# A long-convolution and linear-attention kernel: two blocks of high rows summed by accumulating transfers, numerators scaled straight from PSUM, one-bank spectra tiles, new order lists

## The chip, the cores and the metric

One core of a Trainium2 chip runs the whole kernel. The metric is device time of one execution in microseconds (us). A core has five engines with queues of their own: TensorE (PE, matrix products into PSUM), VectorE (DVE), ScalarE (ACT), GpSimd (POOL) and SyncE (SP, which only issues transfers). Each works through its queue in order and waits on semaphores for the others. SBUF is the working memory with 128 partitions; PSUM holds TensorE's results in banks of 512 fp32 columns.

## The reference

Two independent halves, written side by side into one output of 2048 x 896.

```python
def _A_ref(x, wqkv, w_phi, wo):            # x: 1 x 2048 x 448, 16 heads of 28
    q, k, v = ...                          # x @ wqkv, split into heads
    pq, pk = q @ w_phi, k @ w_phi          # by head
    phi_q = concat(softmax(pq), softmax(-pq))
    phi_k = concat(softmax(pk), softmax(-pk))
    kv, z = einsum("bhsf,bhsd->bhfd", phi_k, v), phi_k.sum over s
    num = phi_q @ kv
    den = phi_q . z + 1e-6
    return (num / den, heads joined) @ wo

def _B_ref(u, A_re, A_im, B_re, B_im, C_re, C_im, log_dt, Dskip):   # u: 1 x 2048 x 448, 256 states
    dt = exp(log_dt); logdA = dt * (A_re + 1j * A_im); dB = dt * (B_re + 1j * B_im)
    P = exp(logdA[:, :, None] * l)         # l = 0 .. 2047, rounded to bfloat16
    K = einsum("dn,dnl,dn->dl", C, P, dB).real
    y = irfft(rfft(pad(u)) * rfft(pad(K)))[:2048]
    return y + u * Dskip
```

## The kernel before

**Convolution kernel K.** The 448 channels go in eight chunks of 56 channels (k = 0..7). A power P at position l is a product of a low and a high factor. For the low rows (W, 50 of them) a chunk's angles are multiplied on TensorE, ScalarE takes Exp of the damping (`dampings`) and Sin of the angle (`rotations`) from PSUM, and VectorE multiplies them (`damp`). The high rows (U, 32 of them, real and imaginary part each) are made on VectorE in `hi_tables` from H (four rows) by complex products with stored powers PW: rows 8 to 11 by PW[256], rows 4 to 7 and 12 to 15 by PW[128], then rows 16 to 23, 24 to 27 and 28 to 31 by PW[512] = (cosine part, sine part). A product with PW[512] is three VectorE instructions: one that multiplies each source row by both parts into a scratch tile t2 (its width is four times the rows' number times 112 columns), a subtraction and an addition. `build_k` multiplies U and W on TensorE in two halves of 112 small matmuls each, and a copy brings each half to SBUF (Ts). `table(k)` is damp and build of chunk k. U, W and E have two buffers, taken in turn by k.

**Spectra.** `scatter_k` moves finished rows of K by many small transfers into Kt; `kernel_spectrum` multiplies them by DFT tables on TensorE (units ks0, ks1, ks2 for three groups of channels: chunks 0 to 3, 4 to 5, 6 to 7). `signal_spectrum` does the same for u in two halves of the sequence: each of 16 steps fills a two-bank PSUM tile "arg" with two results of 448 columns, one copy of 896 columns brings both to SBUF, and transfers write them to DRAM. For the second half of u, one sum of mirrored rows is made by an accumulating transfer on GpSimd's queue (`accum_op`).

**Convolution.** `conv_group` multiplies the spectra of a group on VectorE, `inverse` transforms back on TensorE, copies bring the result to SBUF, and SP writes it out.

**Attention.** `key_pair` and `key_end` make the sums over keys. `query(sc, ...)` handles 512 queries: Exp of the projections, denominators (SC holds their scaled reciprocals, by head), then for each of four blocks of 128 (units q0.0 to q3.3) the numerators in PSUM, their product with SC into `on`, a transpose that adds the two halves, the output projection, and a store. In blocks sc 0 and 1 the product with SC reads PSUM on VectorE. In blocks 2 and 3 (`late`) ScalarE first copies the numerators to SBUF as bfloat16, and VectorE multiplies there by a bfloat16 SC.

**Order.** Every piece of work is a unit with a number in order of the program text and a planner's price for each engine that can do it. The order of all units, with the engine of each, stands in a list written out by hand (`ORDER`: "48A" is unit 48 on ScalarE), and the PSUM tag of each PSUM tile in `PLACES` (a: "arg", two banks; k: "kb"; m: "mm", one bank; two buffers each). The prices are used by nothing at run time. Many copies may run on ScalarE or VectorE; the list says which.

The lines that profile rows name: 347 is VectorE's products and sums (`tt`), 360 ScalarE's activations, 364 its copies (`acopy`), 370 copies on either engine, 380 matmuls, 395 transfers, 709 the negation in `damp`, 842 and 845 reciprocals.

Of the kernel before, what the change touches and what calls it, by code (L numbers as in the profile page):

```python
# [23 lines left out]
N_EARLY = 2  # L24
# [18 lines left out]
HI = ([32 * a for a in range(16)] + [512 + 64 * a for a in range(8)] + [1024 + 128 * a for a in range(8)])  # L43
# [21 lines left out]
def _dft_tables():  # L65
# [27 lines left out]
    for hh in range(4):  # L93
# [3 lines left out]
ORDER = ("0A 48A 3S 1S 2S 4S 8G 23G 13S 25P 46P 36P 30P 32P 47P 44P 29P 17G 193G 27P 49V 50V 53V 51V 192S 19G 52V 54P 55V "  # L97
         "56P 58P 59V 43P 60P 57A 67A 65V 61V 64A 63A 62A 26P 66A 31P 82P 40P 28P 80P 68V 83V 6S 72A 71A 81V 173P 174V "
         "167P 151P 168V 152V 157P 158V 169P 185S 14S 170V 5S 153P 154V 194V 20G 155P 41P 42P 45P 7S 9S 156V 34P 35P 171P "
         "15S 86P 195V 73V 75A 74A 172A 69A 87A 196P 76V 33P 84P 85A 78A 21S 88P 197P 91P 93V 97P 90V 198A 89V 92V 113V "  # L100
         "98V 202P 203P 123P 94P 121P 12S 199S 201G 200G 111A 110A 22G 208P 209P 11S 112V 99V 124A 204A 77A 96V 122V 95V "
         "117V 101V 100V 210A 119P 220P 120A 205S 206G 207G 125P 39P 126A 115A 214P 159P 163P 165P 166A 161P 164A 160A "
         "162A 116V 215P 221P 118A 103V 147P 415P 148V 211S 212S 213S 222A 216A 135P 145P 435P 146A 102V 79V 438A 418A "
         "417A 437A 136V 105V 440P 232P 443A 104V 70V 233P 143P 144V 18S 10S 16S 129P 420P 421P 127P 130V 106V 442A 451P "
         "141P 107V 128V 191G 224G 223S 225S 422A 234A 424A 423A 142V 260P 179P 425P 181P 137P 180V 182V 114A 441P 175P "
         "426V 138V 109V 108V 236G 218S 283G 436P 282A 444A 133P 268A 266A 176A 439A 416P 275A 277A 278A 419A 279A 272A "
         "149P 273A 271A 134V 284V 427P 131P 431P 150V 428V 432V 139P 132V 140V 445P 286V 446V 447P 219G 183G 190G 184G "
         "217G 430P 434P 429P 433P 285V 452V 456P 287V 448V 289V 288V 290V 261A 263A 281A 280A 264A 262A 267A 274A 276A "
         "226P 227P 455P 269A 265A 270A 459V 228A 238P 239P 460P 244P 450P 458A 457A 462A 463A 461P 449P 465P 246A 248A "
         "464A 454P 254A 257A 258A 247A 231G 230S 229S 240A 291V 292V 293V 294V 466V 364G 188G 235S 186S 259A 256A 467P "  # L110
         "453P 480P 296V 295V 300P 468V 297V 483A 253A 482A 356V 299V 298V 475P 478A 309A 477A 301A 249A 471P 472V 485P "
         "363S 339S 237S 469P 340V 486V 342V 487P 470P 488V 341V 252A 304A 251A 312A 302A 474P 245A 306A 476P 365V 255A "
         "479A 343V 481P 484A 315A 303A 250A 307A 310A 627P 491P 473P 358V 345V 344V 492V 311A 630A 313A 314A 308A 621P "
         "177P 626P 623A 305A 624A 629A 628A 178A 489P 346V 493P 316P 321A 337A 241G 324A 642P 490P 242G 366G 622P 645A "
         "326A 320A 329A 325A 322A 333A 317A 318A 243S 189G 357V 338A 319A 336A 328A 327A 330A 373P 374P 334A 335A 331A "
         "332A 631P 347V 323A 625V 349V 348V 375A 359P 350V 632V 377G 352V 351V 551V 553A 360A 361P 367P 368P 369A 353V "
         "511P 529A 533A 530A 514A 362A 513A 526A 525A 633P 552V 516A 522A 515A 532A 385P 521A 528A 523A 386P 354V 355V "
         "535V 512A 518A 517A 524A 531A 527A 519A 520A 554P 634V 371G 537V 536V 538V 372S 378S 534S 376S 387A 540V 539V "
         "541V 555V 556P 557A 646P 379P 380P 649A 648A 542V 543V 544V 545V 495P 501A 370S 505A 510A 641P 635P 494P 637P "
         "636P 643A 504A 644A 507A 509A 496A 381V 651P 546V 547V 638V 558P 653P 548V 652V 550V 549V 654V 598V 503A 560A "  # L120
         "569A 508A 640P 657P 639P 498A 506A 570A 497A 667P 563A 670A 597S 383S 658V 600V 599V 655P 647P 564A 562A 650A "
         "499A 502A 565A 662P 389G 390S 388S 614V 571A 500A 559A 568A 665A 573A 661P 659P 681P 656P 666P 572A 664A 663A "
         "683A 561A 687P 660P 567A 566A 574P 669A 668A 684A 671P 596A 588A 576A 578A 601V 616V 603V 615V 602V 690V 604V "
         "672V 586A 677P 673P 605V 674V 607V 606V 617P 678V 619P 581A 594A 595A 575A 583A 589A 608V 584A 593A 580A 577A "
         "579A 585A 582A 618V 686P 609V 620A 591A 587A 590A 592A 682P 688A 685A 397P 398P 384G 382G 610V 763V 391P 392P "
         "399A 819P 689A 393A 675P 676P 691P 723P 679P 611V 764V 831A 612V 613V 824A 830A 692V 827A 821A 832A 834A 829A "
         "693P 765V 766P 825A 680P 747V 748V 749V 694V 750V 752V 751V 767V 753V 746S 768P 823A 820A 754V 769V 816S 790G "
         "775G 828A 826A 833A 822A 756V 755V 395S 778S 396S 402G 738A 732A 724A 697P 730A 731A 739A 744A 891P 403P 404P "
         "696P 698V 700P 882P 791S 745A 740A 695P 699P 734A 742A 757V 726A 737A 759V 758V 704V 760V 705V 761V 762V 727A "
         "725A 741A 729A 728A 743A 736A 733A 735A 702V 409P 410P 885P 893A 892A 883A 774G 400G 394G 859V 860V 861V 886A "  # L130
         "887A 884A 888P 889A 890A 703V 706V 862V 701V 405A 941P 894P 935P 858S 813S 401S 781S 411A 943A 942A 900P 901P "
         "938P 932P 908P 909P 936A 937A 939A 793G 940A 934A 933A 864V 863V 865V 895V 896V 897V 898V 899V 902V 903P 916P "
         "904A 917P 910V 911P 912A 707P 715A 712A 713A 722A 809S 788S 716A 717A 817G 721A 944P 38P 866V 407G 772S 811S "
         "918V 905P 924P 925P 406G 408G 789G 800G 777G 1282S 802G 945V 946V 947V 770G 714A 926V 906A 709A 786S 795S 187S "
         "776S 818S 808S 710A 720A 718A 719A 711A 708A 919P 1171P 913P 1165P 948V 867V 949V 950P 951P 914A 875V 920A 1172A "
         "1173A 1167A 1166A 907S 810S 927P 958P 959P 921P 922A 928A 952V 835P 804S 960V 876V 37P 961P 801S 836A 1219P 953P "
         "839A 954A 929P 974P 414S 787S 915S 798S 796G 806G 815G 807G 975P 844A 930A 814G 783S 782S 955P 855A 877V 785S "
         "773G 797G 779G 780S 812S 803S 771G 805G 799G 878P 868V 837A 845A 853A 843A 842A 840A 850A 962V 848A 784S 841A "
         "838A 857A 849A 852A 846A 851A 854A 869V 847A 856A 880P 976V 966P 967P 871V 870V 1038V 923S 879A 956A 872V 874V "
         "873V 968V 982P 1168P 1162P 1093P 881A 1039V 1022V 1040V 1220A 991A 1170A 1169A 1221A 1216P 1225P 1164A 1023V "  # L140
         "1024V 1222P 1163A 1107A 1218A 987A 1174P 1175V 1217A 994A 1041P 1104A 1108A 1096A 1098A 1101A 1099A 1025V 1176V "
         "1283S 957S 1021S 1270S 931S 1276S 794S 986A 792S 1227A 1223A 1105A 995A 993A 992A 1226A 1095A 989A 997A 1102A "
         "996A 988A 1043P 1027V 1156V 1026V 1042V 1028V 1177V 1029V 1031V 1271S 413S 1030V 1103A 1277S 1272P 963P 1044A "
         "1100A 1178V 1288S 1032V 964V 1033V 1224A 1034V 1106A 983A 985A 990A 984A 1278P 1279V 1273A 1189P 1190P 977P "
         "1274P 1280P 1094A 1132G 412G 1097A 998P 1035V 1179V 978A 1191A 1281A 1086S 1081S 1054G 1068G 1062G 1053S 1058S "
         "965S 1087S 1036V 1037V 1275V 1133V 1059G 1294S 1017A 1295S 1052S 1289S 1056G 1051G 1091G 1084S 1071G 1300S 1079S "
         "1092S 1228P 1229V 1018A 1016A 1007A 1001A 969P 1003A 999A 1284P 1285A 1135V 1134V 970V 971P 1180P 1004A 1002A "
         "972A 1015A 1011A 1072G 1075G 1065G 1286P 1161S 1067S 1000A 1014A 1008A 1230V 1061G 1049G 1082G 1066G 973S 1306S "
         "1077S 1301S 1136V 979P 1192V 1137V 1138V 1287V 1055G 1046G 1073G 1080G 1139V 1149V 1290P 24P 1181P 1012A 980A "
         "1291A 1010A 1231V 1019A 1006A 1009A 1005A 1020A 1013A 1193P 1296P 1297A 1182A 1292P 1207P 1298P 1151A 1208P "  # L150
# [144 lines left out]
def kernel(  # L295
# [104 lines left out]
    oEND = oF + 61672  # L400
    oT2 = oEND + 4096
    DSK = sb("DSK", [128, D_MODEL], BF16, oDSK)
    PID = sb("PID", [128, 8, 128], BF16, oPID)
    H = sb("H", [128, 4, 2, NCOL], BF16, oH)
    AT = sb("AT", [128, 2, NCOL], BF16, oAT)
    TH = sb("TH", [128, 2, NCOL], BF16, oTH)
# [729 lines left out]
```

## Time and profile before

| | us |
|---|---|
| median of 3 runs | 296.07 (295.61 to 296.17) |
| the profiled execution, its own time | 295.46 |
| its span, first to last instruction | 293.7 |
| VectorE idle before its first instruction | 4.66 |
| VectorE's last convolution step ends | 283.9 |
| TensorE's last matmul ends, about | 290 |

The profile's mean of an instruction is its length from start to end; neighbours on one engine overlap, so a queue's progress is read from start to start. The parts in busy time are those of the engines' compute; waiting and issuing do not count. TensorE ran at a mean granted clock of 0.986. The transfer engines are 10% to 50% busy for most of the span and fuller in the first 25 us and after 200 us:

```profile
PEclk9899999999999999999999999999999989999999
DMA  6985602364003210100432223547886747695033
```

Each digit is one fortieth of the span, in tenths: the clock granted to TensorE, and the mean busy share of 16 transfer engines.

### The profile page before, as it was taken

What the parts mean: (1) busy time and instruction counts of PE and PEld (TensorE: products, weight loads), DVE (VectorE), ACT (ScalarE), POOL (GpSimd) and SP (SyncE); (2) the same over time, 40 slices, a digit from 0 to 9 for tenths busy, and PEclk for the clock granted to TensorE, in tenths of its full rate; (3) what the DMA queues carried; (4) which work ended last, traced back from release to release, by engine and by line L of the source; (5) the groups of instructions that cost most, each with busy time, mean ns of one, the idle gap of its engine ahead of it and who ended that gap; (6) DMA issues with size and microseconds to landing.
All of it is one profiled execution on the core that took longest, in us unless ns stands there. A gap on an engine that the chain in (4) does not pass through costs nothing.

```text
span 293.7 us, 10074 instructions
## 1 busy us (share of the span) xinstructions
PE 252.4 (86%) x4280; PEld 203.5 (69%) x4280; DVE 275.4 (94%) x334; ACT 249.6 (85%) x535; POOL 70.6 (24%) x119
## 2 busy tenths in 40 slices
PE   7688979987988888899789898968678899989994
PEld 2445666775777757868457676957577789879984
DVE  2799999999999999999999999999999999999980
ACT  3999999999999999999999999999999467533421
POOL 4013003412010200000737300089400099000000
PEclk9899999999999999999999999999999989999999
DMA  6985602364003210100432223547886747695033
GB/s 185 283 251 143 192 11 57 101 198 58 7 13 88 58 40 0 33 7 4 83 80 49 41 53 96 123 91 198 296 241 204 253 102 192 171 303 195 2 127 125
DMA packets 40727, 34.91 MB, mean 119 GB/s; under 512 B 22314, under 2 KB 37921, under 8 KB 40555
## 3 DMA queue, kind: packets, MB, share of 16 engines
q1 hardware_dynamic: 35641, 30.37, 35.8%
q0 software_dynamic: 4160, 3.89, 6.8%
q8 instruction: 33, 0.54, 0.7%
q10 hardware_dynamic: 882, 0.02, 0.2%
q14 instruction: 11, 0.09, 0.1%
HBM read 24.02 MB, written 7.34 MB: 107 GB/s over the span
## 4 chain that ended last, share of the span: by engine, by line
ACT 36%; DVE 36%; PE 13%; issue 6%; DMA 5%; SPq 3%; ACTq 0%; DVEq 0%
DVE sbuf L347 30%; ACT sbuf L360 28%; ACT sbuf L370 5%; PE mm L380 5%; PE kb L380 4%; PE arg L380 4%; DMA sbuf<-in_A_wqkv_dram 3%; DVE sbuf L370 3%; SPq L395 3%; ACT L360 2%; DMA sbuf<-sbuf 2%; DVE sbuf L351 1%; DVE sbuf L842 1%; ACT sbuf L709 1%; DVE sbuf L845 0%
## 5 line engine op out<-in xcount | busy, mean ns | idle before, releaser
L380 PEld LDWEIGHTS <-sbuf 128*32 128x32 bf16 (+4 forms) x4056 | 190.7, 119 | 78.5 <-issue 38.4
L347 DVE TENSOR_TENSOR sbuf<-sbuf 128x896 bf16<-128x896 bf16 (+9 forms) x213 | 221.1, 1079 | 2.3 <-ACT sbuf L364 0.7
L380 PE MATMUL mm<-sbuf 128*32 128x50 bf16 (+11 forms) x1901 | 110.4, 261 | 18.1 <-ACT sbuf L360 6.0
L360 ACT ACTIVATE sbuf<-arg 128x224 bf16<-128x224 f32 (+5 forms) x302 | 121.2, 664 | 0.3 <-PE arg L380 0.2
L380 PE MATMUL kb<-sbuf 128*32 128x50 bf16 (+9 forms) x1457 | 81.7, 247 | 7.5 <-issue 2.6
L380 PE MATMUL arg<-sbuf 128*128 128x112 bf16 (+4 forms) x698 | 69.4, 249 | 7.9 <-ACT sbuf L360 4.7
L395 POOL DMA_DIRECT2D sbuf<-sbuf x77 | 46.5, 633 | 103.8 <-issue 38.1
L370 ACT CAST sbuf<-mm 128x448 bf16<-128x448 f32 (+4 forms) x53 | 33.9, 671 | 11.1 <-PE mm L380 7.0
L370 ACT CAST sbuf<-kb 128x448 bf16<-128x448 f32 (+3 forms) x46 | 27.9, 645 | 15.7 <-PE kb L380 14.8
L395 POOL DMA_DIRECT2D SUd<-sbuf x23 | 16.7, 726 | 72.7 <-ACT sbuf L370 69.8
L360 ACT ACTIVATE sbuf<-mm 112x512 bf16<-112x512 f32 x46 | 28.1, 711 | 0.1
L370 ACT CAST sbuf<-arg 128x896 bf16<-128x896 f32 (+2 forms) x27 | 19.4, 747 | 6.4 <-PE arg L380 4.4
L360 ACT ACT_TABLE_LOAD x14 | 18.0, 1283 | 1.4 <-PEq L1120 1.2
L360 ACT ACTIVATE sbuf<-sbuf 128x896 f32<-128x896 f32 (+3 forms) x13 | 12.6, 1013 | 1.9 <-DMA sbuf<-in_B_log_dt_dram 1.9
L347 DVE TENSOR_TENSOR sbuf<-arg,sbuf 128x896 bf16<-128x896 f32 (+1 forms) x10 | 9.7, 988 | 0.1
L364 ACT CAST sbuf<-arg 128x896 bf16<-128x896 f32 x8 | 8.3, 1052 | 1.0 <-PE arg L380 0.9
L347 DVE TENSOR_TENSOR sbuf<-mm,sbuf 128x896 bf16<-128x896 bf16 (+1 forms) x15 | 8.8, 593 | 0.1
L796 PEld LDWEIGHTS <-sbuf 112*128 112x128 bf16 x128 | 7.4, 97 | 2.1 <-issue 1.7
L796 PE MATMUL mm<-sbuf 112*128 112x112 bf16 x112 | 7.8, 212 | 1.1 <-ACT sbuf L370 0.6
L364 ACT CAST sbuf<-sbuf 128x1792 bf16<-128x1792 f32 (+1 forms) x5 | 7.2, 1430 | 0.0
L360 ACT ACTIVATE sbuf<-kb 112x512 bf16<-112x512 f32 x12 | 7.0, 667 | 0.0
L370 DVE CAST sbuf<-arg 128x224 bf16<-128x224 f32 (+1 forms) x4 | 2.2, 560 | 4.8 <-ACT sbuf L370 4.8
(39 smaller groups left out, 82.2 us busy)
## 6 DMA issues: line engine op xcount, KB each, us to landing
sbuf<-const SPq DMA_DIRECT2D x36, 224.0 KB
sbuf<-const SPq DMA_DIRECT2D x6, 512.0 KB
sbuf<-in_B_u_dram SPq DMA_DIRECT2D x6, 448.0 KB
sbuf<-in_A_x_dram SPq DMA_DIRECT2D x4, 448.0 KB
out_dram<-sbuf SPq DMA_DIRECT2D x16, 112.0 KB
sbuf<-SUd SPq DMA_DIRECT2D x1, 1792.0 KB
sbuf<-SUd SPq DMA_DIRECT2D x2, 896.0 KB
out_dram<-sbuf SPq DMA_DIRECT2D x8, 224.0 KB
```

The lines of the kernel that those rows point to most:

```text
L347: lambda: nc.vector.tensor_tensor(out=at(out_), in0=at(a), in1=at(b), op=op), [whose(a), whose(b)], [out_])
L351: lambda: nc.vector.scalar_tensor_tensor(out=at(out_), in0=at(a), scalar=sc, in1=at(b), op0=op0, op1=op1),
L360: lambda: nc.scalar.activation(at(out_), at(a), func, scale=scale, bias=bias),
L364: plan.add({"ACT": 0.09 + count(out_) * 0.833e-3}, lambda: nc.scalar.copy(at(out_), at(a)), [whose(a)], [out_])
L370: lambda e: (nc.scalar.copy if e == "ACT" else nc.vector.tensor_copy)(at(out_), at(a)), [whose(a)], [out_])
L380: nc.tensor.matmul(out_, lhsT=lhsT, rhs=rhs, start=start, stop=stop, **kw)
L395: plan.add({e: own[e] for e in engs}, lambda e=engs[0]: QUEUES[e].dma_start(out=out_, in_=in_, **kw), r, w, lat=lat, load=pieces / 16000 * ...
L709: lambda en: nc.scalar.mul(m, m, -1.0) if en == "ACT" else nc.vector.tensor_scalar_mul(m, m, -1.0), [m], [m])
L796: mms(pt, [lambda t, i=i, s=s, c=c: nc.tensor.transpose(t[:, s, 112 * c:112 * c + 112], EKT[:, s, c, 128 * i:128 * i + 128], id112) for s ...
L842: plan.add({"DVE": 0.87}, lambda: nc.vector.reciprocal(rz[:, :, :, :], at(ndv(1))), [pz], [rz[:, :, :, :]])
```

## The change

1. High rows (`hi_tables`): the order of U's rows is changed (HI), so that the block of eight rows (16 to 23) becomes two of four: rows 16 to 19, from every fourth row, and rows 20 to 23. The last two blocks (24 to 27 and 28 to 31) stay four rows each. Two of the six blocks (20 to 23 and 28 to 31) are made in another way: VectorE multiplies the source by a new tile SN = (sine, -sine) into a scratch tile with real and imaginary part swapped, multiplies the source by the cosine into the rows, and an accumulating transfer on GpSimd's queue adds the scratch tile to the rows. SN is made once for a chunk by two products of 112 columns (unit sn).
2. PID, the scaled identity matrices, loses its first matrix, for which the plain identity is used; SN lies in the bytes.
3. u's spectra: each result of 448 columns has a one-bank tile "mm" of its own and a copy of its own, 32 for 16.
4. Numerators: the late branch goes. A unit may run on VectorE as one product from PSUM, or on ScalarE as 32 activations, one for each head and sign, with that head's SC as scale. SC is fp32 always.
5. ORDER and PLACES are new. Of copies that can run on either engine, some changed sides; loads and small transfers changed places between SP's and GpSimd's queues.

The change is described as "Two of six blocks of high rows summed by accumulating DMA, all numerators scaled straight from PSUM on VectorE, one-bank tiles for u's spectra, new order lists".

```diff
-HI = ([32 * a for a in range(16)] + [512 + 64 * a for a in range(8)] + [1024 + 128 * a for a in range(8)])
+HI = ([32 * a for a in range(16)] + [512 + 128 * a for a in range(4)] + [576 + 128 * a for a in range(4)] + [1024 + 128 * a for a in range(8)])
...
-    PID = sb("PID", [128, 8, 128], BF16, oPID)
+    PID = sb("PID", [128, 7, 128], BF16, oPID)
+    SN = sb("SN", [128, 2, COLS], BF16, oPID + 3584)
...
-                    p = ps("arg", [128, 2, 512])
                     for k2 in range(2):
                         mt = 2 * mp + k2
+                        p = ps("mm", [128, 512])
...
-                    copy(sg[:, :, :], (p, lambda t: t[:, :, 0:D_MODEL]))
+                        copy(sg[:, k2, :], (p, lambda t: t[:, 0:D_MODEL]))
...
-        for lv, (j, dst, src, n) in enumerate(((256, u[:, 8:12], H, 4), (128, None, u[:, 8:12], 4),
-                                               (512, u[:, 16:24], u[:, 0:16:2], 8), (512, u[:, 24:28], u[:, 16:24:2], 4),
-                                               (512, u[:, 28:32], u[:, 24:28], 4))):
+        step(f"sn{k}", rank)
+        sine = PW[512][:, 1, cols]
+        for r, f in enumerate((1.0, -1.0)):
+            plan.add({"ACT": 0.15, "DVE": 0.11}, lambda e, r=r, f=f: nc.scalar.mul(SN[:, r, :], sine, f) if e == "ACT" else
+                     nc.vector.tensor_scalar_mul(SN[:, r, :], sine, f), [sine], [SN[:, r, :]])
+        for lv, (j, dst, src, tmp) in enumerate(((256, u[:, 8:12], H, None), (128, None, u[:, 8:12], None),
+                                                 (512, u[:, 16:20], u[:, 0:16:4], None),
+                                                 (512, u[:, 20:24], u[:, 2:16:4], 3584),
+                                                 (512, u[:, 24:28], u[:, 16:20], None),
+                                                 (512, u[:, 28:32], u[:, 24:28], 5376))):
             step(f"hi{k}.{lv + 1}", rank)
-            t2 = times(j, src, n)
+            if tmp:
+                t2 = sb("tm", [128, 4, 2, COLS], BF16, oT2 + tmp)
+                tt(t2[:, :, ::-1, :], src, SN.unsqueeze(1).to_broadcast([128, 4, 2, COLS]), ALU.mult)
+                tt(dst, src, PW[512][:, 0, cols].unsqueeze(1).unsqueeze(1).to_broadcast([128, 4, 2, COLS]), ALU.mult)
+                dma(["POOL"], dst, t2[:, :, :, :], r=[t2[:, :, :, :], dst], w=[dst], lat=6, cost=0.85, accum_op=ALU.add)
+                continue
+            t2 = times(j, src, 4)
...
-            if late:
-                acopy(on[:, :, :], (pn, lambda t: t[:, :, 0:D_MODEL]))
-            tt(heads, heads if late else (pn, lambda t: t[:, :, 0:D_MODEL].rearrange("p s (h d) -> p s h d", d=D_HEAD)),
-               SC[:, t4].unsqueeze(3).to_broadcast([128, 2, 16, D_HEAD]), ALU.mult)
+            def scaled(e, pn=pn, heads=heads, SC=SC, t4=t4):
+                if e == "DVE":
+                    nc.vector.tensor_tensor(out=heads, in0=num(pn.t), op=ALU.mult,
+                                            in1=SC[:, t4].unsqueeze(3).to_broadcast([128, 2, 16, D_HEAD]))
+                    return
+                for s in range(2):
+                    for h in range(N_HEAD):
+                        nc.scalar.activation(heads[:, s, h], num(pn.t)[:, s, h], ACT.Copy, scale=SC[:, t4, s, h:h + 1])
+            plan.add({"ACT": 2.6, "DVE": 0.065 + 2 * D_MODEL * 1.04e-3}, scaled, [pn, SC[:, t4]], [on[:, :, :]])
```

## The prediction

> **What bounds the kernel now.** I read the engines' busy times first, then three stretches, then VectorE's and ScalarE's instructions by shape, then the timeline round the last table.
>
> ```profile
> span 293.7 us, 10074 instructions
> PE 252.4 (86%) x4280; PEld 203.5 (69%) x4280; DVE 275.4 (94%) x334; ACT 249.6 (85%) x535; POOL 70.6 (24%) x119
> ...
> core 0: us, PE busy (x) PEld busy (x) DVE busy (x) ACT busy (x) POOL busy (x), PEclk, DMA share, GB/s
> 12.00:228.00 216.00, 186.56 (x3253) 146.35 (x3254) 213.51 (x277) 214.30 (x469) 52.11 (x83) 0.99 0.38 99
> 228.00:285.00 57.00, 53.70 (x926) 49.76 (x918) 56.10 (x45) 26.82 (x56) 15.16 (x26) 0.97 0.57 168
> 285.00:293.70 8.70, 4.56 (x76) 4.31 (x73) 0.59 (x2) 1.41 (x3) 0.00 (x0) 0.92 0.40 136
> ```
>
> From 12 to 228 us VectorE and ScalarE are both full (213.5 and 214.3 of 216). From 228 on ScalarE is half idle, while VectorE is full (56.1 of 57) and TensorE nearly (53.7). So two engines share the bound in each part, and an edit pays only where both move.
>
> ```profile
> L347 DVE TENSOR_TENSOR sbuf<-sbuf 128x1792 bf16<-128x1792 bf16 x47 | 50.3, 1079 | 0.2
> L347 DVE TENSOR_TENSOR sbuf<-sbuf 128x896 bf16<-128x896 bf16 x66 | 43.3, 674 | 1.4 <-ACT sbuf L364 0.7
> L347 DVE TENSOR_TENSOR sbuf<-sbuf 128x3584 bf16<-128x3584 bf16 x20 | 40.1, 2013 | 0.0
> L347 DVE TENSOR_TENSOR sbuf<-sbuf 128x448 bf16<-128x448 bf16 x48 | 16.3, 376 | 0.1
> L347 DVE TENSOR_TENSOR sbuf<-arg,sbuf 128x896 bf16<-128x896 f32 x8 | 8.5, 1082 | 0.1
> L364 ACT CAST sbuf<-arg 128x896 bf16<-128x896 f32 x8 | 8.3, 1052 | 1.0 <-PE arg L380 0.9
> L360 ACT ACT_TABLE_LOAD x14 | 18.0, 1283 | 1.4 <-PEq L1120 1.2
> ```
>
> A queue advances from start to start, and VectorE's starts are some 80 ns closer than these means: 1.935 (3584 columns), 1.002 (1792), 0.536 (896), 0.302 (448), 1.001 us (896 from PSUM). On ScalarE the median distances are 0.143 us for 112 columns, 0.237 for 224, 0.423 for 448, 0.785 to 0.797 for 896.
>
> ```profile
> 44.11 0.26 ACT L360 ACTIVATE sbuf<-arg 128x112 bf16<-128x112 f32 x1
> 44.27 0.53 ACT L370 CAST sbuf<-mm 128x448 bf16<-128x448 f32 x1
> 44.68 0.81 ACT L360 ACTIVATE sbuf<-arg 128x448 bf16<-128x448 f32 x2
> ...
> 217.04 1.08 DVE L347 TENSOR_TENSOR sbuf<-sbuf 128x896 bf16<-128x896 bf16 x1
> 235.85 1.08 DVE L347 TENSOR_TENSOR sbuf<-sbuf 128x896 bf16<-128x896 bf16 x1
> ...
> 227.24 2.74 PE L380 MATMUL mm<-sbuf 128*32 128x50 bf16 x112 [0.75 <-DVE sbuf L347]
> 229.73 1.24 PE L380 MATMUL kb<-sbuf 128*32 128x50 bf16 x43
> 232.41 1.82 PE L380 MATMUL kb<-sbuf 128*32 128x50 bf16 x69 [1.44 <-issue]
> ```
>
> The 0.26 us activation is followed after 0.16. The two 1.08 us lines are late numerators scaled from SBUF: eight of the 66 cost as much as one read from PSUM, 1.00 from start to start, so ScalarE's copy ahead of them bought nothing. Last, TensorE waits for VectorE to damp table 7 (until 227.1), builds it, and is full from there to 290.
>
> **The change by parts, on VectorE.** Sums go over the two lists, start to start.
> High rows: a chunk's last levels cost 1.935 + 2x0.536 + 2x(1.002 + 2x0.302) = 6.22 and now 2x(1.002 + 2x0.302) + 4x0.536 = 5.36; 0.86 by eight chunks is -6.9.
> SN: 16 products of 112 columns, 11 on VectorE. No row has this size in 128 partitions; 112x16 copies take 172 - 80 = 92 ns and 112x112 scalings 247 - 80 = 167, so 0.14: +1.5; five on ScalarE at 0.143: +0.7.
> Numerators: the change is described as putting all of them on VectorE, but the new lists put twelve there and four (the last two of query blocks 2 and 3) on ScalarE: in this it doesn't do what it says. Eight late ones at 1.00 become four at 1.00: -4.0, of which -1.0 ahead of table 7.
> u's spectra: seven 448-column copies of 0.532 for one of 1.00: +2.7.
> Other copies that changed engine, summed by row: -2.6 ahead of table 7, -2.2 in all.
> To the end of table 7's damping: -6.9 + 1.5 - 1.0 + 2.7 - 2.6 = -6.3. To VectorE's last convolution step: -6.9 + 1.5 - 4.0 + 2.7 - 2.2 = -8.9.
>
> **ScalarE.** Up to table 7's last rotation its list shrinks by 3.5 us (15 copies of 0.785 become 25 of 0.424, and fewer others), and the built program has 10 table loads for 14, all ahead of that point: 4 x 1.28 = 5.1. So rotations come 8.6 earlier and VectorE asks for them 6.3 earlier. This is the cover of the 6.3; if it failed by more than 2.3, table 7 would be late by the rest.
>
> **The four numerators on ScalarE**: each is 32 activations of 28 columns with a scale that is read from SBUF, an operand that no activation of the trace has. Below, the line through 112 to 896 columns (0.05 + 0.00083 a column) gives 0.073 and a unit of 2.3 us. Above, the only tiny activation (112x4, nothing behind it) is busy 0.205: 6.6 us. I take 0.143, the shortest distance of two ScalarE starts anywhere in this trace: a unit L = 4.6. Held behind them on ScalarE: after the first two, both copies of table 7; after each of the others, the copies of the kernel spectra that the second convolution group needs, and a two-bank PSUM tile that an inverse transform waits for. Laying the rows out in list order from table 7's damping: the pair may take 8.3 us before TensorE misses table 7's banks, the third unit 3.9 (six PE items of 0.2 to 1.73), the fourth 2.3. Held: (2L - 8.3) + (L - 3.9) + (L - 2.3) = 4L - 14.5 = 3.9, with 0 and 11.9 as ends. The two builds took 6.9 instead of 2x2.5 before; I keep that stall of TensorE's own, and the first wait hides behind its 1.9: 2.0 left.
> By the Trainium skill (ScalarE: Activation LUTs, What ACT_TABLE_LOAD costs) each pointer operand adds about 93 ns to an activation. That would be an estimated 0.166, a unit of 5.3 and 4.8 held; its figure without pointers (93 ns overlap on 186 + 0.833 a column) gives more than this trace's 0.05 + 0.00083 a column, so it is not trusted outright.
>
> **TensorE's tail.** After table 7 the new list leaves 1.6 more: two halves of 0.22, a transpose of 0.45, an output product of 0.76. Its waits on VectorE in the tail (0.52, 0.19) should go, as VectorE runs 8.9 ahead there: -0.7. The rest stays.
>
> **Priced at nothing.** 16 accumulating transfers: the trace has one of 448 KB, 1.44 us on GpSimd and 5.5 us to land, and plain ones of 224 KB at 4.7. 16 issues are 12 to 23 us on an engine that is 24% busy; behind each stand plain pieces of scatter and spectra. For chunk 7 VectorE has 0.43 + 0.14 + 1.83 + 2x1.0 + 4.04 = 8.4 us to do before the build may start: 2.9 to spare. For chunk 2 only 2.6 lie between, so build 2 waits 2.9; TensorE has 8 us idle in 100 to 150 for it. Without that cover: 3 to 4 us late, once. Loads: up to wqkv and the first half of u SP's queue has the same 2.4 MB in both lists; then x's fourth block and PID (0.67 MB) pass the B matrices, which at the 250 GB/s of the first slices land 2.7 later, while VectorE asks for them 2 later and had some 4 to spare: 0; without it, 1. The copies of H for chunks 1 and 6 move to GpSimd's queue, chunk 7's to SP's, each wanted over 10 us later: 0. The one-bank spectra tiles: two starts instead of one, within a TensorE that is idle 29 us before 228; 0 to 2.
>
> **Sum.** Span 293.7 - 6.3 + 1.6 - 0.7 + 2.0 = 290.3 by TensorE; by VectorE 293.7 - 8.9 = 284.8 plus at most 4, earlier. -3.4 on the profiled 295.46 us gives 292.1; the median 296.07 is 0.6 above that run, so **292.5** between the two readings of it (292.1 and 292.7).
>
> **Rivals.**
> 1. The small activations run at the line's 0.073: nothing held, -5.4: 290.7; if TensorE's own stalls go with it, down to VectorE's -8.9: 287.2. I write 289. For: the medians of all four sizes lie on that line. Against: none has a scale from memory.
> 2. The operand half shows: 0.174, midway between 0.143 and 0.205, L = 5.6: held 7.9 - 1.9 = 6.0, +0.6: 296.7, no change. By the Trainium skill's pointer rule (the page and section above) the time would be an estimated 295.4, just short of this.
> 3. Slower: ScalarE's four units at 0.205, L = 6.6, ahead of table 7's copies: held 11.9 - 1.9 = 10.0, -5.4 + 10.0 = +4.6: 300.7. It decides from 0.17 a piece (4L - 16.4 = 5.4, L = 5.45). For: ScalarE alone frees those banks and its order is fixed. Against: it is idle half of the tail.
> 4. The gain lies off the path: rotations, or U's summed rows, come late for the tables and table 7 is damped at 227 as before: -6.3 gone, +0.9 + 2.0: 299. For: ScalarE was as full as VectorE, and sixteen landings are new. Against: 8.6 us off ScalarE, 2.9 to spare.
>
> **Chances.** Forecast 0.45 (own range 289.5 to 295.3); rival 1 0.20; rival 2 0.13; rival 3 0.13; rival 4 0.09. About 0.2% (0.6 us) is what a measurement tells from no change. Faster: nearly all of the forecast, rival 1, half of rival 2: 0.42 + 0.20 + 0.07 = 0.69 with a little from the others, 0.70. Same: 0.02 + 0.05 + 0.03 = 0.10. Slower: 0.20. The range, 287.5 to 298.0, leaves out some of rival 1 and most of 3 and 4.
>
> **What would show it.** VectorE's 3584-column products fall from 20 to 12 and its damping of table 7 ends near 221; 128 ScalarE activations of 28 columns, whose start distance says which of 0.073, 0.143 and 0.205 holds; ten table loads; TensorE full from about 221 with waits on ScalarE of some 2 us. It is wrong if VectorE shows waits for ScalarE or for a landing between 60 and 220, or if TensorE is idle by more than 5 us after table 7.

## The result and the profile after

| | before | after |
|---|---|---|
| median, runs side by side on one chip (us) | 295.61 (294.88 to 296.69, 7 runs) | 297.86 (297.43 to 298.67, 7 runs) |
| ratio to before, 95% interval | | 1.0073 [1.0052, 1.0093] |
| span of the profiled execution (us) | 293.7 | 296.0 |
| mean granted clock of TensorE | 0.986 | 0.976 |

The change makes the kernel 0.73% slower. The forecast was 3.6 us faster. Medians and ranges here and below are of all runs; ratios leave out runs more than 1.5% above the fastest of their kernel, a slower state that some executions of any kernel fall into. The mean granted clock doesn't order the seven runs after: 297.46 us at 0.977 and 297.72 at 0.988, 297.43 at 0.969 and 298.67 at 0.971. The page of the kernel after, its span and engines:

```profile
span 296.0 us, 10282 instructions
PE 253.8 (86%) x4280; PEld 205.1 (69%) x4280; DVE 266.4 (90%) x355; ACT 259.5 (88%) x666; POOL 89.5 (30%) x143
```

VectorE has 9.0 us less work (275.4 before), ScalarE 9.9 more (249.6 before), GpSimd 18.9 more. The stretches tell where that lies. Columns as in the prediction; first two stretches of the kernel before:

```profile
12.00:220.00 208.00, 179.75 (x3133) 140.36 (x3134) 205.51 (x272) 206.44 (x455) 52.11 (x83) 0.99 0.37 96
220.00:285.00 65.00, 60.51 (x1043) 55.75 (x1035) 64.10 (x50) 34.68 (x73) 15.16 (x26) 0.97 0.57 171
```

and the kernel after:

```profile
12.00:220.00 208.00, 185.43 (x3188) 145.56 (x3191) 203.53 (x296) 204.85 (x473) 69.14 (x104) 0.98 0.48 113
220.00:285.00 65.00, 53.47 (x943) 49.40 (x943) 53.28 (x40) 44.93 (x180) 17.01 (x29) 0.97 0.58 168
285.00:296.00 11.00, 6.46 (x101) 6.04 (x99) 3.63 (x8) 1.48 (x4) 0.00 (x0) 0.97 0.33 112
```

Ahead of 220 TensorE did 5.7 us more than before. Between 220 and 285 it did 7.0 us less at the same granted clock of 0.97, VectorE 10.8 less, and ScalarE 10.3 more. What was gained ahead of 220 is idle time behind it. The instructions by shape, for after (busy time, mean ns of one, idle time ahead and what ended it):

```profile
L349 DVE TENSOR_TENSOR sbuf<-sbuf 128x896 bf16<-128x896 bf16 x74 | 44.1, 617 | 0.5
L349 DVE TENSOR_TENSOR sbuf<-sbuf 128x3584 bf16<-128x3584 bf16 x12 | 23.8, 2021 | 6.1 <-ACT sbuf L372 5.3 <-DMA sbuf<-SUd 0.8
L878 DVE TENSOR_TENSOR sbuf<-arg,sbuf 128x896 bf16<-128x896 f32 x12 | 13.0, 1085 | 5.8 <-issue 3.5 <-PE mm L382 1.9 <-PE arg L382 0.5
...
L883 ACT ACTIVATE sbuf<-arg,sbuf 128x28 bf16<-128x28 f32 x128 | 22.9, 509 | 0.0
L362 ACT ACT_TABLE_LOAD x10 | 12.8, 1283 | 1.3 <-PEq L1144 1.2
```

The 3584-column products fell from 20 to 12, twelve numerators are on VectorE, four are 128 activations on ScalarE, and there are ten table loads. The mean of 509 ns is the length of one pipelined activation and says little; the timeline of ScalarE round table 7 gives the pace:

```profile
219.88 0.58 ACT L372 CAST sbuf<-kb 128x448 bf16<-128x448 f32 x1
220.30 11.39 ACT L883 ACTIVATE sbuf<-arg,sbuf 128x28 bf16<-128x28 f32 x64
231.00 1.51 ACT L372 CAST sbuf<-mm 128x350 bf16<-128x350 f32 x2
232.54 2.24 ACTq L397 DMA_DIRECT2D sbuf<-sbuf  x2
...
242.20 5.72 ACT L883 ACTIVATE sbuf<-arg,sbuf 128x28 bf16<-128x28 f32 x32
```

From 220.30 to 231.00 are 10.70 us for two units: 5.35 a unit, 0.167 from start to start (the median of the single starts is the same). The 128x350 copies behind them are table 7's; the ACTq row is ScalarE's queue issuing two transfers. TensorE's side of it, idle time and its releaser in brackets:

```profile
226.29 1.37 PE L382 MATMUL mm<-sbuf 128*32 128x50 bf16 x52 [2.27 <-issue]
232.17 1.90 PE L382 MATMUL mm<-sbuf 128*128 128x112 bf16 x24 [2.36 <-ACT sbuf L372]
235.84 0.75 PE L382 MATMUL mm<-sbuf 128*128 128x112 bf16 x12 [1.37 <-ACT sbuf L372]
247.98 1.89 PE L382 MATMUL arg<-sbuf 128*128 128x224 bf16 x18 [2.13 <-ACT sbuf L883]
255.99 1.89 PE L382 MATMUL arg<-sbuf 128*128 128x224 bf16 x18 [3.40 <-ACT sbuf L883]
```

The 2.27 are a stall inside the build of table 7. Then come two waits for copies that stand behind the first pair of units (the second of them also behind the two transfers), and two for the two-bank tile that the third and the fourth unit hold: 2.36 + 1.37 + 2.13 + 3.40 = 9.3 us. VectorE waits for the same units. In its view of waits (total, times, longest):

```profile
DVE sbuf L349 <- ACT sbuf L372: 5.3, 2, 4.7
```

The 4.7 stands ahead of the second convolution group, whose spectra ScalarE copies late.

### The profile page after: what moved, and what is told of

It is laid out like the page before. It is cut to its first block, busy times and chain, and to the rows that moved or that the text cites. A ratio compares the mean times of both kernels' runs of the same rounds, so it can differ in the third digit from the quotient of the medians.

```text
span 296.0 us, 10282 instructions
## 1 busy us (share of the span) xinstructions
PE 253.8 (86%) x4280; PEld 205.1 (69%) x4280; DVE 266.4 (90%) x355; ACT 259.5 (88%) x666; POOL 89.5 (30%) x143
## 5 line engine op out<-in xcount | busy, mean ns | idle before, releaser
L349 DVE TENSOR_TENSOR sbuf<-sbuf 128x896 bf16<-128x896 bf16 (+8 forms) x213 | 205.9, 1010 | 6.8 <-ACT sbuf L372 5.3
L382 PE MATMUL mm<-sbuf 128*32 128x50 bf16 (+11 forms) x2574 | 154.1, 265 | 19.7 <-ACT sbuf L372 12.9
L362 ACT ACTIVATE sbuf<-arg 128x224 bf16<-128x224 f32 (+5 forms) x310 | 134.6, 662 | 0.1
L397 POOL DMA_DIRECT2D sbuf<-sbuf x101 | 66.9, 786 | 88.2 <-DVE sbuf L349 23.9
L372 ACT CAST sbuf<-mm 128x448 bf16<-128x448 f32 (+4 forms) x94 | 58.2, 655 | 15.7 <-PE mm L382 15.0
L382 PE MATMUL kb<-sbuf 128*128 128x112 bf16 (+10 forms) x900 | 65.9, 242 | 3.8 <-issue 1.3
L382 PE MATMUL arg<-sbuf 128*128 128x112 bf16 (+4 forms) x582 | 44.9, 228 | 8.5 <-ACT sbuf L883 5.5
L372 ACT CAST sbuf<-kb 128x448 bf16<-128x448 f32 (+4 forms) x37 | 22.6, 640 | 6.7 <-DMA out_dram<-sbuf 3.1
L883 ACT ACTIVATE sbuf<-arg,sbuf 128x28 bf16<-128x28 f32 x128 | 22.9, 509 | 0.0
L878 DVE TENSOR_TENSOR sbuf<-arg,sbuf 128x896 bf16<-128x896 f32 x12 | 13.0, 1085 | 5.8 <-issue 3.5
```

The source lines that it names most:

```text
L349: lambda: nc.vector.tensor_tensor(out=at(out_), in0=at(a), in1=at(b), op=op), [whose(a), whose(b)], [out_])
L362: lambda: nc.scalar.activation(at(out_), at(a), func, scale=scale, bias=bias),
L372: lambda e: (nc.scalar.copy if e == "ACT" else nc.vector.tensor_copy)(at(out_), at(a)), [whose(a)], [out_])
L382: nc.tensor.matmul(out_, lhsT=lhsT, rhs=rhs, start=start, stop=stop, **kw)
L397: plan.add({e: own[e] for e in engs}, lambda e=engs[0]: QUEUES[e].dma_start(out=out_, in_=in_, **kw), r, w, lat=lat, load=pieces / 16000 * ...
L878: nc.vector.tensor_tensor(out=heads, in0=num(pn.t), op=ALU.mult, in1=SC[:, t4].unsqueeze(3).to_broadcast([128, 2, 16, D_HEAD]))
```

## The experiments

Each ran against the kernel before on the same chip. The medians of the kernel before lie between 295.61 and 297.26 us, so kernels are compared by their ratio to before.

| run | numerators q2.2, q2.3 / q3.2, q3.3 | median (range, runs) | before there | ratio [95%] |
|---|---|---|---|---|
| the change | ScalarE / ScalarE | 297.86 (297.43 to 298.67, 7) | 295.61 | 1.0073 [1.0052, 1.0093] |
| e3_imm_scale | ScalarE, constant scale | 290.67 (289.91 to 295.16, 4) | 296.45 | 0.9794 [0.9740, 0.9847] |
| e1_num_dve | VectorE, same places | 298.82 (298.49 to 301.68, 6) | 296.45 | 1.0123 [1.0073, 1.0172] |
| e2_num_dve_late | VectorE, first pair behind table 7 | 295.79 (293.63 to 299.64, 12) | 296.45 | 0.9990 [0.9959, 1.0021] |
| e4_before_direct | (the kernel before, late copies left away) | 304.58 (303.62 to 306.27, 6) | 296.45 | 1.0286 [1.0244, 1.0329] |
| e5_num_dve_spread | as e2, q3.3 earlier | 291.81 (290.08 to 294.22, 6) | 296.71 | 0.9840 [0.9782, 0.9897] |
| e6_num_copy_dve | as e2, ScalarE copies first | 290.61 (289.04 to 293.96, 6) | 296.71 | 0.9796 [0.9745, 0.9848] |
| e7_no_accum | as e5, no accumulating transfers | 297.59 (295.94 to 299.69, 12) | 296.71 | 1.0037 [1.0000, 1.0075] |
| e8_first_pair_dve | VectorE behind table 7 / ScalarE | 295.35 (290.98 to 297.97, 6) | 297.26 | 0.9873 [0.9797, 0.9950] |
| e9_copy_spread | as e6, q3.3 earlier | 292.04 (289.99 to 295.59, 11) | 297.26 | 0.9803 [0.9765, 0.9841] |

Profiles of kernels with the same list up to table 7 differ by up to 4 us in when they reach it (its damping ends at 217.8 in e2 and at 222.2 in e5). Of these 4.4 us, 2.8 are there already at the first table's damping (68.9 and 71.7): TensorE's first products with wqkv, which wait for its load, start at 10.65 in e2 and at 12.57 in e5. So waits are read inside one trace, and times from the ratios; where the ends of two traces are compared below, they carry this uncertainty.

### The price of the scale operand: e3_imm_scale

```diff
-                        nc.scalar.activation(heads[:, s, h], num(pn.t)[:, s, h], ACT.Copy, scale=SC[:, t4, s, h:h + 1])
+                        nc.scalar.activation(heads[:, s, h], num(pn.t)[:, s, h], ACT.Copy, scale=1.0)
```

The scaling of the four numerator blocks is left out; the 128 activations, their places and every wait stay.

> The change with an immediate scale of 1.0 in its 128 activations of 28 columns; the scaling of four numerator blocks is left out. It tells whether the 0.179 us between two starts is the price of a small activation or of the operand read from SBUF. If of the operand: distance 0.073 (the line through 112 to 896 columns), units of 2.3 us, and the time 6 to 8 us below the change, 290 to 292. If of any small activation (0.143 or more): units of 4.6 or more and at most 3 to 4 us below the change.

ScalarE's timeline in e3:

```profile
220.83 5.55 ACT L883 ACTIVATE sbuf<-arg 128x28 bf16<-128x28 f32 x64
225.81 1.00 ACT L372 CAST sbuf<-mm 128x350 bf16<-128x350 f32 x1
```

and TensorE's, in the places of the four waits above:

```profile
227.43 1.37 PE L382 MATMUL mm<-sbuf 128*32 128x50 bf16 x52 [2.92 <-issue]
...
230.75 2.95 PE L382 MATMUL mm<-sbuf 128*128 128x112 bf16 x24
...
233.93 0.76 PE L382 MATMUL mm<-sbuf 128*128 128x112 bf16 x12
...
244.20 1.89 PE L382 MATMUL arg<-sbuf 128*128 128x224 bf16 x18
...
249.05 1.89 PE L382 MATMUL arg<-sbuf 128*128 128x224 bf16 x18
```

The same 64 activations take 4.98 us to the next start (225.81 - 220.83) instead of 10.70, with a median distance of 0.074. TensorE's four waits on ScalarE are gone (these four rows have no brackets); the stall inside the build, which waits for nothing shown, stays (2.92). From 220 to 285 TensorE does 61.28 us of work, against 53.47. The time goes from 1.0073 to 0.9794 of before: leaving out one operand read from SBUF, 128 times, gave back 2.8%, some 8 us, and everything else in the change is worth 2.1%. The ratio of e3 rests on three runs, and its interval reaches half a per cent to either side.

### The numerators where the description puts them: e1 and e2

e1 puts the four units on VectorE and leaves them in their places; e2 also moves the first two behind the last product that table 7 needs.

```diff
 e1:
-1253P 1254A 1262A 1367V 1369P ... 1461P 1304A 1427G ... 1462A 1312A 1292A
+1253P 1254V 1262V 1367V 1369P ... 1461P 1304V 1427G ... 1462A 1312V 1292A
 e2:
+1253P 1367V 1254V 1262V 1369P ... 1461P 1304V 1427G ... 1462A 1312V 1292A
```

> The change with its four ScalarE numerators put on VectorE, at the same places of the order list. Theory (the hold behind ScalarE's small activations gives the gain back): ScalarE loses 4 units of 5.7 us, VectorE gains 4 x 1.0, two of them ahead of table 7's damping, which ends 2.0 later than in the change (near 221.8); the waits for the PSUM tiles and copies behind the units (some 8 us) go. Time 3 to 5 us below the change, so 293 to 295. Rival (the tail is TensorE's own and table 7's end alone sets it): 2 us above the change, near 300. Rival (the gain is lost to transfers, which are the same here): the change's time within 1 us.

> As the run before, but the first two of the four numerators stand behind table 7's damping on VectorE, so that table 7 is damped as early as in the change (219.8). Theory: 5 to 7 us below the change, 291 to 293, and 1 to 2 below the run before. Rival (TensorE's tail alone): the change's time. Rival (transfers): the change's time within 1 us.

Both missed. ScalarE is free of the units, and new waits take their place. VectorE's timeline in e1:

```profile
220.16 2.09 DVE L878 TENSOR_TENSOR sbuf<-arg,sbuf 128x896 bf16<-128x896 f32 x2 [4.22 <-PE arg L382]
222.17 4.11 DVE L349 TENSOR_TENSOR sbuf<-sbuf 128x7616 bf16<-128x7616 bf16 x1
```

VectorE reaches the pair 4.22 us before TensorE has it, and table 7's damping stands behind that wait. From the end of table 6's damping to the end of table 7's are 25.2 us in e1, 20.6 after the change and 19.1 in e2: the wait and the pair cost e1 4.6 of what the change had gained there. Later TensorE also waits for the last numerator in e1:

```profile
255.59 3.49 PE L382 MATMUL arg<-sbuf 128*128 128x224 bf16 x18 [3.64 <-DVE sbuf L878]
```

In e2 the first wait is gone (damping 213.72 + 4.12 = 217.8), but the last numerator is late too. TensorE's timeline in e2:

```profile
249.23 3.15 PE L382 MATMUL arg<-sbuf 128*128 128x224 bf16 x16 [4.38 <-DVE sbuf L878]
```

and VectorE's:

```profile
241.03 7.15 DVE L349 TENSOR_TENSOR sbuf<-sbuf 128x7168 bf16<-128x7168 bf16 x4
248.09 1.08 DVE L878 TENSOR_TENSOR sbuf<-arg,sbuf 128x896 bf16<-128x896 f32 x1
```

The unit stands behind 7 us of convolution products, its two-bank tile stays taken until 249.2, and TensorE waits 4.38 for it. So moving the work off the slow operand is not enough: here a PSUM tile was held just as long by a fast instruction that stood late in a full queue.

### Freeing the tile in time: e5, e6 and e9

e5 is e2 with unit 1312 right behind 1304. e6 is e2 with a ScalarE copy ahead of each product; e9 is e6 with 1312 right behind 1304.

```diff
 e5, e9:
-1461P 1304V 1427G ... 1462A 1312V 1292A
+1461P 1304V 1312V 1427G ... 1462A 1292A
 e6, e9:
+                    src = num(pn.t)
+                    if (sc, t4 // 2) in ((2, 1), (3, 1)):
+                        nc.scalar.copy(on[:, :, :], pn.t[:, :, 0:D_MODEL])
+                        src = heads
-                    nc.vector.tensor_tensor(out=heads, in0=num(pn.t), op=ALU.mult,
+                    nc.vector.tensor_tensor(out=heads, in0=src, op=ALU.mult,
```

> As e2 (all sixteen numerators on VectorE, the first two of the last four behind table 7's damping), with the last one (q3.3) moved on VectorE from behind 10 us of convolution steps to right behind q3.2. Theory (what counts in the tail is how long a two-bank PSUM tile of numerators is held, by whichever engine reads it late): TensorE's inverse transform no longer waits for q3.3's tile, the copies of ks1 come 4 us earlier, the wait of 4.54 us ahead of the second group's first product on VectorE goes, and the time is 3 to 4.5 us below e2: 291 to 293. Rival (the tail is bound by TensorE's own work): e2's time.

> As e2, but for the last four numerators ScalarE first copies the PSUM tile to SBUF (0.8 us, as the kernel before did) and VectorE scales there at e2's places. The PSUM tile is free after the copy instead of after VectorE's product. Theory (the hold of the tile): 3 to 4 us below e2, near e5. Rival (ScalarE's copy buys nothing, as the prediction said): e2's time or up to 1 us above it.

> e6 (copies by ScalarE, products on VectorE) with q3.3 moved to right behind q3.2 on VectorE, as in e5. The tile is already freed by the copy, so theory: within 1 us of e6. Rival (VectorE's place for q3.3 still counts, since its transpose is queued on TensorE): 1 to 3 us below e6.

In e5 VectorE takes both numerators of block 3 ahead of the long products:

```profile
241.09 2.08 DVE L878 TENSOR_TENSOR sbuf<-arg,sbuf 128x896 bf16<-128x896 f32 x2
243.09 9.94 DVE L349 TENSOR_TENSOR sbuf<-sbuf 128x7168 bf16<-128x7168 bf16 x4
```

With that one unit moved, e5 is at 0.984 where e2 is at 0.999. e6 leaves the unit late and is at 0.980: a copy on an engine that has time there brings the tile free. ScalarE's copy, TensorE's next use of the tile and VectorE's product in e6:

```profile
246.76 0.93 ACT L880 CAST sbuf<-arg 128x896 bf16<-128x896 f32 x1
250.71 1.89 PE L382 MATMUL arg<-sbuf 128*128 128x224 bf16 x18
253.94 1.08 DVE L882 TENSOR_TENSOR sbuf<-sbuf 128x896 bf16<-128x896 bf16 x1
```

VectorE multiplies 7 us after the copy, and TensorE starts in between without a wait. e9 moves the unit too and shows no gain over e6 (0.9803 and 0.9796): once the tile is free, when VectorE multiplies makes no difference that these intervals, half a per cent to either side, could show. e5, e6 and e9 compute all of it and beat both kernels, by 1.6 to 2.0% against before. Their intervals overlap, so no order among the three is claimed.

### Which pair costs what: e8_first_pair_dve

```diff
-1253P 1254A 1262A 1367V 1369P ... 1304A ... 1312A
+1253P 1367V 1254V 1262V 1369P ... 1304A ... 1312A
```

> The change with the first two of its four ScalarE numerators (q2.2, q2.3) on VectorE behind table 7's damping; q3.2 and q3.3 stay on ScalarE. It parts the loss between the two pairs. By the trace of the change TensorE waits 2.13 and 3.40 us for the tiles of q3.2 and q3.3, and the first pair holds table 7's copies to 231 to 232.5. Theory: table 7's copies come near 226 to 227, and the time is 3 to 4 us below the change; the rest of the way to e5 (some 2 to 3 us) is the second pair's. Rival (only the second pair costs): the change's time.

TensorE's timeline in e8 has the two waits of the units that are left on ScalarE, and neither of the other two:

```profile
244.75 1.89 PE L382 MATMUL arg<-sbuf 128*128 128x224 bf16 x18 [2.12 <-ACT sbuf L883]
...
252.05 1.89 PE L382 MATMUL arg<-sbuf 128*128 128x224 bf16 x18 [2.68 <-ACT sbuf L883]
```

The ratio goes from 1.0073 to 0.9873: 2.0%, 5.9 us, for the first pair, more than the 3 to 4 expected and more than its two waits on TensorE (3.7). But the ratio rests on three runs and its interval is 4.5 us wide; the medians of all runs give 0.994, a gain of 1.4%. So how the 8 us divide between the pairs is not settled. That each pair costs something is: 2.12 and 2.68 remain in e8 with only the second there.

### Is the early copy of before worth anything: e4_before_direct

The kernel before, with the late numerators multiplied straight from PSUM on VectorE and the eight ScalarE copies left away:

```diff
-        SC = sb("SCb", [128, 4, 2, 16], BF16, ...) if late else sb("SC", [128, 4, 2, 16], F32, ...)
+        SC = sb("SC", [128, 4, 2, 16], F32, ...)
...
-                acopy(on[:, :, :], (pn, lambda t: t[:, :, 0:D_MODEL]))
-            tt(heads, heads if late else (pn, ...), SC..., ALU.mult)
+                plan.add({"ACT": 0.0}, lambda: None, [pn], [on[:, :, :]])
+            tt(heads, (pn, ...), SC..., ALU.mult)
```

(The units of the copies stay in the list and do nothing.)

> The kernel before with its eight late numerators scaled straight from PSUM on VectorE, no copy by ScalarE; order and all else as before. VectorE's products cost the same 1.0 us, ScalarE loses eight copies of 0.8. Theory (ScalarE in order ahead of the tail's copies matters): 0 to 2 us below before. If copies in ScalarE's idle tail cost nothing: no change within 0.6 us.

It is 2.9% slower, though VectorE's instructions cost the same from PSUM and ScalarE has less to do. TensorE's and ScalarE's rows in its view of waits:

```profile
PE arg L380 <- DVE sbuf L347: 13.0, 6, 6.5
...
ACT sbuf L360 <- PE arg L380: 8.3, 3, 7.7
```

and the longest of them in TensorE's timeline:

```profile
220.28 2.51 PE L380 MATMUL arg<-sbuf 128*128 128x112 bf16 x24 [6.47 <-DVE sbuf L347]
```

TensorE waits 13.0 us for two-bank tiles that VectorE has not read yet, ScalarE waits 8.3 for the angles that TensorE then brings late, and table 7's damping ends at 234.8 instead of 227.2. So in this order ScalarE's copy bought the tile's early release.

### The accumulating transfers: e7_no_accum

```diff
-                dma(["POOL"], dst, t2[:, :, :, :], r=[t2[:, :, :, :], dst], w=[dst], lat=6, cost=0.85, accum_op=ALU.add)
+                tt(dst, dst, t2[:, :, :, :], ALU.add)
```

on top of e5, the sixteen units on VectorE in the same places.

> As e5, with the 16 accumulating transfers replaced by additions of 896 columns on VectorE (0.54 us each, 8.6 in all). If the accumulating transfers do what they are for and land in time: table 7 is damped 8 to 9 us later than in e5 and the time is 6 to 9 us above it. Rival (their landings or GpSimd's queue cost the tables as much as they save): within 2 us of e5.

The ratio rises from 0.9840 to 1.0037, 2.0% or 5.8 us, a little short of the 6 to 9 expected. The sixteen additions take 8.5 us of VectorE's starts ahead of table 7's damping (0.53 each), and VectorE is idle there for 3.8 us less than in e5 (9.1 and 12.9). So this part of the change is worth about 2%. The line of the transfers in the change (KB each, median us from issue to landing), with the sixteen and three plain ones:

```profile
sbuf<-sbuf POOLq DMA_DIRECT2D x19, 224.0 KB, 3.7
```

## Why the prediction was wrong, point by point

**What bounds the kernel.** It held: an edit pays where both engines of a stretch move. The edit moved VectorE and left TensorE's banks with ScalarE.

**VectorE, -6.3 to the end of table 7's damping.** Measured -7.4 (227.2 to 219.8) in one trace each; e3, with the same list, reached that point at 220.3. The counts were right: twelve 3584-column products, twelve numerators.

**ScalarE's cover, 8.6 of 6.3.** It held: table 7's last rotation ended 8.3 earlier (222.3 to 214.0), with ten table loads. Rival 4, a gain off the path, falls with it, since table 7 was not damped at 227 as before.

**The four numerators on ScalarE: this step failed.** "I take 0.143, the shortest distance of two ScalarE starts anywhere in this trace: a unit L = 4.6" took a row of 112 columns for a lower limit of 28-column work, and then priced the operand at what was left. The runs show two terms: 0.074 without the operand, where the line through the larger sizes says 0.073, and 0.093 for the operand. Together 0.167 and L = 5.35. The line and the operand were the way to the number, and the nearest row was not. The Trainium skill's rule (ScalarE: Activation LUTs, What ACT_TABLE_LOAD costs: about 93 ns for each pointer operand, one that is read from memory) agrees with 0.167 - 0.074 = 0.093 to the nanosecond. Added to this trace's own line it gives an estimated 0.166, the figure that the prediction set aside because another term of that page of the Trainium skill did not fit. That other term (186 + 0.833 a column, less 93 of overlap) is an estimated 0.84 us for 896 columns; in the trace before, such activations start 0.84 us apart where they read SBUF and 0.80 where they read PSUM, and the prediction had compared it with PSUM rows alone.

**What is held behind them: sized too small as well.** In the sum this term stood at 2.0 us; TensorE's four waits are 9.3.

| place | predicted term, L = 4.6 | same term, L = 5.35 | TensorE's wait |
|---|---|---|---|
| copies of table 7, behind the build's own stall | 2L - 8.3 - 1.9 = -1.0 | 0.5 | 2.36 |
| a second wait behind them | not seen | not seen | 1.37 |
| third unit | L - 3.9 = 0.7 | 1.45 | 2.13 |
| fourth unit | L - 2.3 = 2.3 | 3.05 | 3.40 |
| sum | 2.0 | 5.0 | 9.3 |

The cover of the first place was right: TensorE gets to its wait 10.05 us after table 7's damping (232.17 - 2.36 - 219.76), its stall included, against 8.3 + 1.9 = 10.2. But ScalarE lets go later than after 2L. Its first activation starts 0.54 after the damping, the 64 take 10.70, and TensorE goes on 1.17 after the start of the first copy (232.17 - 231.00); the 0.54 and the 1.17 stand in no term. (At its own L the prediction also let a stall of 1.9 hide a wait of 0.9 and counted the 1.0 left over as a gain.) The second wait is for copies behind the two transfers that ScalarE issues from 232.54 to 234.78, right after table 7's. The third and the fourth unit hold their tile until their last activation ends, 5.7 us after the first starts and not 5.35, which is most of what these two terms lack. Of the 7.3 us that were missing, 3.0 are the price of the activation, 1.9 the first place, 1.4 the second wait and 1.0 the last two.

**TensorE's tail and the sum.** No wait of TensorE on VectorE is left in the tail, as said. The predicted span was 290.3; +7.3 held and -1.1 at table 7 give 296.5, and 296.0 was measured. The prediction's own sign of being wrong, TensorE idle by more than 5 us after table 7, was there.

**Priced at nothing.** The transfers cost no wait that decides: the sixteen land 3.2 to 6.1 us after their issue where 5.5 was assumed, and the last of chunk 7, the slowest, lands at 217.1, ahead of the build at 219.9. The waits shown on TensorE's side for transfers within SBUF are 0.6 us in all, so the 2.9 assumed for build 2 did not come, and the only wait of VectorE's products for a transfer is one of 0.8 for a spectrum's load in the tail. "ScalarE's copy ahead of them bought nothing" was wrong, by e4: the remark compared the instructions' lengths and left out who waits for the tile. It entered no term, but it is the same blindness as in the failed step, a price for the engine's time and too short a one for the bank.

**The rivals.** The mechanism that came true is that of rivals 2 and 3, the operand's price. By price it was rival 2 (0.174, no change); by outcome rival 3 (slower), whose point of decision, L = 5.45, was set too high, since it left out the same held time. Rival 1's condition, no time for the operand, is what e3 makes: it forecast 289, and e3 at 0.9794 of 296.07 is 290.0.

**The description.** As the prediction noted, four numerators are not on VectorE. Putting them there in the same places is no better (e1, 1.012, with an interval that overlaps the change's), and putting them there in good places is better (e5, 0.984).

## What to carry to other kernels

Price an instruction that the trace lacks by its parts, the size's own line plus a term for each operand that comes from memory, and not by the nearest whole row. A unit that reads a PSUM tile has two prices, its engine's time and the time until the tile is free; the second counted in full here, where TensorE has only two such tiles, so a plain early copy on an engine with slack can be worth more than the instruction it adds. In an in-order queue a consumer must stand behind the point where its input is ready and ahead of the next long run of work: moving one 1-us unit past 7 us of products was worth 1.5% here.

## What the runs showed of the hardware that was not expected

- ScalarE pays for a scale read from SBUF at every activation even when 64 follow each other without a gap: 0.167 from start to start against 0.074 with a constant, at 28 columns.
- With a constant, the pace of small activations stays on the line of the large ones down to 28 columns (0.074 measured, 0.073 on the line).
- The sixteen accumulating transfers of 224 KB within SBUF land 3.2 to 6.1 us after their issue, median 3.8. The three plain ones of that size on the same queue take 3.2 in the same run; the two of the kernel before took 5.1 and 4.3.
